# Scaling B and C of three chunk pairs on GpSimd instead of VectorE in a Mamba-2 plus low-rank-mixer kernel

## The chip, the cores and the metric

The kernel runs on one core of a Trainium2 chip. A core has five engines with a queue of instructions each: TensorE (PE in the profile; PEld is its weight load), VectorE (DVE), ScalarE (ACT), GpSimd (POOL) and SyncE (SP, which here only issues transfers). The engines run side by side and wait for one another by semaphores. The metric is the device time of one execution in microseconds (us); lower is better.

## The reference

The inputs are x (4 batches, 8 heads, 768 positions, 32 channels), decays a, and B and C (16 states per head). The first half is a chunked state-space scan; the second half a mixer on its output, as (batch, 768, 256).

```python
cum = np.cumsum(la, axis=-1)
L = np.exp(cum[:, :, :, None] - cum[:, :, None, :])
CB = np.einsum('bhin,bhjn->bhij', Cc, Bc)
M = CB * L * causal
y = M @ xc  +  (C @ state) * exp(cum)
state = exp(sum(la)) * state + sum_j B_j x_j exp(cum_last - cum_j)
...
h = xt @ U @ V
u = x + h.transpose(0, 2, 1)
out = u + np.maximum(u @ w_ch1, 0.0) @ w_ch2
```

The factor L splits: exp(cum_i - cum_j) is exp(cum_i - m) times exp(m - cum_j) for any m. So B may be multiplied by one factor for each position and head and C by another, and after that the masked product of the two is M.

## The kernel before

**Pairs.** The 768 positions of a batch are cut into 6 blocks of 128, taken two at a time: a *pair*. Pairs 0 to 2 belong to the first batch, 3 to 5 to the second, up to 11. For every pair the kernel does these steps, each a function of its own:

- `prep` (L344): the tile `BC` is B and C of the pair times the factors `F` (L271), which are computed for all positions ahead; 128 partitions by 512 columns, both inputs and the output in SBUF. It runs on VectorE. `BC` has two buffers.
- `decayed` (L356): `bd`, B times another factor `FD`, 128x256, on GpSimd.
- `turn` / `turning` (L374): four transposes of BC on TensorE, then ScalarE copies the result into `T` (L378) and, masked by head, `Cm` (L384).
- `gram` (L405): B times C in four PSUM banks of the tags x and z. `mask` (L417, VectorE) makes M of it.
- `state` (L438, TensorE) multiplies bd with x; `update` (L456, L458, VectorE) carries the state on, and L465 (GpSimd) makes `Sm` of it.
- `intra` (L537) and `inter` (L515) are the two products whose sum is y; `yout` (L549) copies y from PSUM.

**Weights.** The mixer's weights come in 64-bit floating point, as pairs of 32-bit words, and are converted piece by piece in `to_fp32`: on VectorE `e` (L315) and `top` (L317), on ScalarE `rest` (L319) and `power` (L321), and on VectorE again L323, L325 and L327 (the last writes the weight). Its scratch tiles have two buffers, so the first ScalarE step of one piece waits until L327 two pieces earlier has read that buffer. `convert_ahead` starts the next piece and then finishes the current one; its DVE order is L315, L317, L323, L325, L327.

**Mixer.** `up` (L701, then a ReLU on ScalarE, L706, into `gT`) and `down` (`whole`, L816) serve the first batch. Later batches use forms with fewer multiplications (L633 and L741). The `up` products use the same x and z banks as `gram`, so a gram has to wait until L706 has read them.

**Order.** The order on every engine is written out by hand: each queue runs its instructions as the program lists them. Pairs 0 to 2 are written out one by one; then the first batch's `up` pieces are interleaved with conversions and with the preparation of pairs 3 and 4:

```python
    prep(3)
    decayed(3)
    convert_ahead()
    ...
    turn(3)
    prep(4)
    decayed(4)
    ...
    gram(3); state(3); mask(3); update(3)
    convert_ahead()
```

From pair 3 on a loop does, for pair k: `prep(k + 2)`, `decayed(k + 2)`, then the mixer pieces of this turn with the four steps of `turning(k + 2)`, then `inter(k)`, `gram(k + 1)`, `intra(k)`, `state(k + 1)`, `mask(k + 1)` and so on. So pair 5 is prepared in the first turn of this loop, ahead of a `convert_ahead`.

SyncE issues all loads in one order fixed at the start. The input tiles `bc` and `x` have six buffers, so the load for pair 9 waits until the steps that read pair 3's tile are done.

Of the kernel before, what the change touches and what calls it, by code (L numbers as in the profile page):

```python
# [20 lines left out]
def kernel(  # L21
# [27 lines left out]
    nc = tc.nc  # L49
# [4 lines left out]
    NPR = NC // 2  # L54
# [284 lines left out]
    def prep(k, c=0, n=2):  # L339

        b, q = pairs[k]
        if c == 0:
            st[k] = {"BC": att.tile([P, 2, 2, NH, N], FP32, tag="BC", name="BC")}
        nc.vector.tensor_tensor(  # L344
            out=st[k]["BC"][:, :, c:c + n].rearrange("p i c h n -> p i (c h) n"),
            in0=bc_sb[k][:, :, c:c + n].rearrange("p i c h n -> p i (c h) n"),
            in1=F[:, :, b, 2 * q + c:2 * q + c + n].rearrange("p i c h -> p i (c h)")[
                :, :, :, None].to_broadcast([P, 2, n * NH, N]),
            op=ALU.mult)
# [555 lines left out]

    decays(one)
    prep(0, 0, 1)
    keep(one, "z")
    turn(0, 0, 1)
    prep(0, 1, 1)  # L910
    decayed(0)
    fill(1)
    turn(0, 1, 1, "w", nc.vector)
    fill(2)
    gram(0)
    prep(1, 0, 1)
    state(0)
    mask(0)
# [185 lines left out]
```

## Time and profile before

| what | us |
|---|---|
| median of 5 runs | 239.96 (239.7 to 241.28) |
| the profiled execution | 240.67 |
| its span, first to last instruction | 238.8 |
| TensorE busy in the span | 228.2 |
| VectorE busy | 155.4 |
| ScalarE busy | 95.5 |
| GpSimd busy | 20.5 |

All positions in the profile are us from the start of the span. The granted TensorE clock was 1.000 of full speed over the span. In a line of the timeline the first number is the start, the second the duration, then engine, source line and operation, output and inputs by the program's names, and in brackets how long the engine had been idle and what released it. An instruction may start a little ahead of the end of the one before it on the same engine. In the list of waits the three numbers are total, times and longest.

### The profile page before, as it was taken

The page shows a single profiled execution, that of the slowest core. Times are in us where ns is not written, and L with a number is a line of the kernel's source. Part 1 is how long each engine was busy: PE and PEld are TensorE (multiplying, and loading weights), DVE is VectorE, ACT ScalarE, POOL GpSimd, SP SyncE. Part 2 cuts the span into 40 slices and gives each one's busy share as a digit, 9 for nine tenths or more (in the row PEclk, how much of TensorE's full clock was granted, in tenths as well). Part 3 has the DMA queues.
Part 4 walks back from the last instruction along what each step waited for, and adds up shares of the span by engine and source line. Part 5 has one row for each costly group of instructions (what it writes and reads, how often), then busy time and mean ns, then how long its engine had stood idle before and what let it go on. Part 6 is the DMA issues. An engine that isn't in the chain of part 4 may idle for free.

```text
span 238.8 us, 7374 instructions
## 1 busy us (share of the span) xinstructions
PE 228.2 (96%) x3166; PEld 175.6 (74%) x3166; DVE 155.4 (65%) x363; ACT 95.5 (40%) x245; POOL 20.5 (9%) x40
## 2 busy tenths in 40 slices
PE   7988799897899999999999999999999999999995
PEld 5666566455688988565799987565799896559994
DVE  3675899798896666475896671556974372478511
ACT  5344647856414212537614112456312014663110
POOL 4221001120330300002021100010000000000000
PEclk9999999999999999999999999999999999999999
DMA  6975949998897830100001010000001011000111
GB/s 82 112 93 149 278 54 299 180 104 103 99 113 94 99 104 0 44 3 3 3 3 47 5 44 22 26 3 0 3 3 47 11 36 44 0 0 3 44 47 45
DMA packets 81909, 14.60 MB, mean 61 GB/s; under 512 B 76052, under 2 KB 80084, under 8 KB 81876
## 3 DMA queue, kind: packets, MB, share of 16 engines
q1 hardware_dynamic: 81876, 14.13, 32.5%
q8 instruction: 25, 0.41, 0.7%
q14 instruction: 8, 0.07, 0.1%
HBM read 10.98 MB, written 3.15 MB: 59 GB/s over the span
## 4 chain that ended last, share of the span: by engine, by line
PE 76%; SPq 10%; DVE 6%; DMA 3%; issue 2%; ACT 2%; DVEq 0%; ACTq 0%
PE x L741 17%; PE x L633 14%; PE z L741 13%; PE z L633 10%; SPq L117 8%; PE y L537 3%; PE x L816 3%; PE y L515 3%; PE x L405 2%; DMA words<-in_moe_w_ch_dram 2%; PE w L586 2%; PE w L557 2%; SPq L126 2%; PE x L737 1%; PE w L438 1%
## 5 line engine op out<-in xcount | busy, mean ns | idle before, releaser
L633 PE MATMUL x<-t,ws 128*128 128x384 f32 x72 | 28.7, 496 | 0.0
L741 PE MATMUL x<-w2s,words 128*128 128x128 f32 x176 | 23.2, 275 | 0.0
L741 PEld LDWEIGHTS x<-w2s,words 128*128 128x128 f32 x176 | 21.6, 193 | 0.0
L621 ACT ACTIVATE gT<-gT 128x384 f32<-128x384 f32 x36 | 19.0, 527 | 2.4 <-DVE gT L642 2.3
L465 POOL TENSOR_TENSOR Sm<-S,slot 128x256 f32<-128x256 f32 (+1 forms) x12 | 8.8, 735 | 121.4 <-DVE S L458 86.5
L633 PEld LDWEIGHTS x<-t,ws 128*128 128x128 f32 x72 | 12.5, 190 | 8.0 <-ACT top L638 1.3
L730 DVE TENSOR_TENSOR words<-gT 128x512 f32<-128x512 f32 (+1 forms) x28 | 16.7, 598 | 0.6 <-ACT gT L621 0.6
L642 DVE TENSOR_TENSOR gT<-z,top 128x384 f32<-128x384 f32 x12 | 6.7, 558 | 15.2 <-PE z L633 13.4
L638 ACT COPY e<-x 128x384 f32<-128x384 f32 x12 | 5.7, 478 | 23.2 <-PE x L633 23.2
L417 DVE TENSOR_TENSOR M<-x,causal 128x256 int32<-128x256 int32 x24 | 9.1, 420 | 9.0 <-PE z L405 7.7
L549 ACT COPY yT<-y 128x256 f32<-128x256 f32 x24 | 7.8, 375 | 16.5 <-PE y L515 16.5
L799 ACT COPY o<-x 128x128 f32<-128x128 f32 x11 | 2.9, 265 | 28.6 <-PE x L741 28.6
L405 PE MATMUL x<-Cm,T 32*64 32x128 f32 x192 | 11.9, 288 | 1.5 <-ACT Cm L384 1.1
L458 DVE SCALAR_TENSOR_TENSOR S<-S,kept,w 128x64 f32<-128x64 f32 x40 | 11.2, 279 | 3.1 <-PE w L438 1.4
L701 PE MATMUL x<-yT,w 128*128 128x384 f32 x32 | 12.0, 497 | 0.7 <-DVE yT L601 0.6
L741 PE MATMUL x<-w,gT 128*128 128x128 f32 x88 | 12.6, 286 | 0.0
L676 DVE TENSOR_SCALAR gT<-x 128x384 f32<-128x384 f32 x12 | 6.7, 557 | 9.1 <-PE x L633 9.1
L741 PEld LDWEIGHTS x<-w,gT 128*128 128x128 f32 x88 | 10.8, 191 | 2.3 <-issue 1.6
L741 PE MATMUL z<-w2s,words 128*128 128x128 f32 x88 | 11.9, 279 | 0.0
L356 POOL TENSOR_TENSOR bd<-bc,FD 128x256 f32<-128x256 f32 (+1 forms) x13 | 9.3, 716 | 30.3 <-ACT FD L282 16.3
L515 PE MATMUL y<-T,Sm 32*64 32x64 f32 x352 | 11.2, 230 | 0.7 <-ACT settled L471 0.4
L701 PE MATMUL z<-yT,w 128*128 128x384 f32 x32 | 11.6, 486 | 0.0
(179 smaller groups left out, 506.1 us busy)
## 6 DMA issues: line engine op xcount, KB each, us to landing
words<-in_moe_w_ch_dram SPq DMA_DIRECT2D x7, 512.0 KB, 6.0
x<-in_x_dram SPq DMA_DIRECT2D x24, 128.0 KB, 3.5
out_dram<-o SPq DMA_DIRECT2D x11, 256.0 KB, 2.1
bc<-in_B_dram SPq DMA_DIRECT2D x24, 64.0 KB, 3.4
bc<-in_C_dram SPq DMA_DIRECT2D x24, 64.0 KB, 2.9
words<-in_moe_w_ch_dram SPq DMA_DIRECT2D x2, 256.0 KB, 3.9
words<-in_moe_V_dram SPq DMA_DIRECT2D x1, 192.0 KB
words<-in_moe_U_dram SPq DMA_DIRECT2D x1, 192.0 KB, 5.0
```

Of the source, the lines that this page charges most:

```text
L117: nc.sync.dma_start(out=bc_sb[k][:, i, c], in_=src[b, :, ts(2 * q + c, P), :].rearrange("h s n -> s h n"))
L356: nc.gpsimd.tensor_tensor(out=st[k]["bd"][:, c:c + n].rearrange("p c h n -> p (c h) n"), in0=bc_sb[k][:, 0, c:c + n].rearrange("p c h n -> ...
L405: nc.tensor.matmul(out=g[r][cols, c], lhsT=s["T"][rows, 0, c, cols], rhs=s["Cm"][rows, :, c, cols], start=(c == 0), stop=True, skip_group_ ...
L417: done = nc.vector.tensor_tensor(out=M[:, r].bitcast(INT32).rearrange("p c s i -> p (c s) i"), in0=g[r].bitcast(INT32).rearrange("p c s i ...
L458: done = nc.vector.scalar_tensor_tensor(out=new, in0=st["S", b], scalar=kept[:, b, j, None], in1=add, op0=ALU.mult, op1=ALU.add)
L465: nc.gpsimd.tensor_tensor(out=s["Sm"][:, sl], in0=s["S"][:, sl].rearrange("p i (s d) -> p i s d", s=2), in1=slot[:, None, :, None].to_broa ...
L515: product = nc.tensor.matmul(out=y[p][ts(r % 2, H), r // 2, c], lhsT=own[ts(r, Q)], rhs=s["T"][ts(r, Q), 1, c, ts(p, H)], start=fresh(k, p ...
L621: nc.scalar.activation(g, g, AF.Relu)
L633: nc.tensor.matmul(out=X[name], lhsT=lhsT[:, ts(i, P)], rhs=rhs, start=start, stop=True, skip_group_check=True)
L701: nc.tensor.matmul(out=g, lhsT=w1[:, n, ts(m, P)], rhs=uT[:, n, ts(k, HS)], start=(n == 0), stop=(n == NCB - 1))
L730: nc.vector.tensor_tensor(out=S[v][:, lo:hi], in0=l[:, lo:hi], in1=r[:, lo:hi], op=op)
L741: nc.tensor.matmul(out=X[name], lhsT=lhsT[:, i], rhs=rhs[:, i], start=start and u is None and i == 0, stop=True, skip_group_check=True)
```

## The change

In `prep` the engine is chosen by the pair: pairs 3, 4 and 5 (`NPR` is 3), which are the second batch, use GpSimd, all others VectorE as before. The shapes, the values and the place in the program stay the same. On GpSimd's queue each of the three stands directly ahead of its pair's `bd`; on VectorE's queue three 128x512 instructions are gone. The source has one line more from there on, so L345 and later of the changed kernel are L344 and later of the kernel before.

```diff
         if c == 0:
             st[k] = {"BC": att.tile([P, 2, 2, NH, N], FP32, tag="BC", name="BC")}
-        nc.vector.tensor_tensor(
+        engine = nc.gpsimd if NPR <= k < NPR + 3 else nc.vector
+        engine.tensor_tensor(
             out=st[k]["BC"][:, :, c:c + n].rearrange("p i c h n -> p i (c h) n"),
             in0=bc_sb[k][:, :, c:c + n].rearrange("p i c h n -> p i (c h) n"),
             in1=F[:, :, b, 2 * q + c:2 * q + c + n].rearrange("p i c h -> p i (c h)")[
```

## The prediction

> **What bounds the kernel now.** I read the busy times first, then the chain of work that ended last, then what TensorE waited for, and last the timeline of the stretch in which the three edited instructions stand (38 to 57 us).
>
> The first and fourth part of the page:
>
> ```profile
> PE 228.2 (96%) x3166; PEld 175.6 (74%) x3166; DVE 155.4 (65%) x363; ACT 95.5 (40%) x245; POOL 20.5 (9%) x40
> ...
> PE 76%; SPq 10%; DVE 6%; DMA 3%; issue 2%; ACT 2%; DVEq 0%; ACTq 0%
> ```
>
> TensorE is the bound, and GpSimd is nearly empty. From about 57 us on, the chain is TensorE practically without a break, so time gained or lost on VectorE counts only where TensorE waits. Those places, from the list of its waits over the whole span:
>
> ```profile
> PE x L405 <- ACT Cm L384: 1.1, 1, 1.1
> PE x L374 <- DVE BC L344: 1.0, 3, 0.4
> ...
> PE w L374 <- DVE BC L344: 0.4, 1, 0.4
> ...
> PE x L405 <- ACT gT L706: 0.3, 1, 0.3
> ```
>
> The first is at 44.92 to 46.03 us (gram of pair 3), the third at 53.84 to 54.27 (turning of pair 5), the fourth at 55.38 to 55.65 (gram of pair 4); the second lies in the first batch and is not touched. So at most 0.43 + 0.27 = 0.70 us of waiting, 0.3% of the span, stands behind the edited lines; the 1.1 us hangs on a transfer, as the chain there shows:
>
> ```profile
> 35.26 4.69 DMA words<-in_moe_w_ch_dram
> 39.95 0.02 issue
> 39.97 0.43 DVE e L315
> ...
> 41.98 0.70 DVE w L327
> 42.68 0.02 issue
> 42.70 0.69 ACT rest L319
> ```
>
> And the timeline, VectorE, GpSimd and ScalarE, where the third edited instruction stands:
>
> ```profile
> 50.22 0.66 POOL L465 TENSOR_TENSOR Sm<-S,slot 128x256 f32<-128x256 f32 x1 [3.73 <-DVE S L458]
> 50.32 0.83 DVE L317 TENSOR_SCALAR top<-words 128x512 int32<-128x512 int32 x1
> 50.84 0.80 POOL L356 TENSOR_TENSOR bd<-bc,FD 128x256 f32<-128x256 f32 x1
> 51.08 1.10 DVE L323 SCALAR_TENSOR_TENSOR rest<-top,rest 128x512 f32<-128x512 f32 x1
> 52.11 0.69 DVE L325 SCALAR_TENSOR_TENSOR power<-words,power 128x512 int32<-128x512 int32 x1
> 52.83 0.69 DVE L327 SCALAR_TENSOR_TENSOR w<-rest,power 128x512 f32<-128x512 f32 x1
> 53.44 0.69 DVE L344 TENSOR_TENSOR BC<-bc,F 128x512 f32<-128x512 f32 x1
> 53.55 0.67 ACT L319 ACTIVATE rest<-words 128x512 f32<-128x512 uint32 x1
> 54.49 0.72 ACT L321 ACTIVATE power<-e,bias 128x512 int32<-128x512 int32 x1 [0.28 <-DVE e L315]
> ```
>
> The reader is to see that L317 takes 0.83 and L323 1.10 beside a running GpSimd instruction, where the same forms take 0.42 and 0.69 elsewhere. L323 ends at 52.18, so its own 0.69 began at 51.49, which is 0.15 before bd ended (51.64); bd in turn took 0.80 instead of 0.62 and began its own 0.62 at 51.02, just before L317 ended (51.15). Two such instructions do not run together: one waits until about 0.14 before the other's end. At 38.45 us a bd took its plain 0.62 beside L292 and L295 of VectorE, also at plain length, so some VectorE forms are free of this; the conversion's (L315 to L327) are not.
>
> **The change, part by part.** It takes three 128x512 instructions of L344 (0.68, 0.69, 0.69 us; the next one starts 0.60 after) off VectorE and puts them on GpSimd, each in front of its pair's bd. No transfer, matmul or ScalarE instruction moves. Loads queued on SyncE that reuse these input buffers (pair 9's first, at 66.12) wait for GpSimd alone instead of both, which has finished more than 20 us earlier: nothing.
>
> *Length on GpSimd.* No row shows 128x512. Bounds: 0.62 (a 128x256) and 2.12 (two 128x256 at the slowest seen, 1.06). GpSimd rows without a wait for the other engine are 0.40 for 128x128, 0.51 for 128x192, 0.62 for 128x256, a straight line of 0.11 per 64 columns; I take the line's 1.06 (an estimate), nearest to the rows.
>
> *Pair 3.* VectorE loses 39.00 to 39.68, but its next instruction waits for the transfer that lands at 39.95: gain 0, the idle time of 0.29 just grows. GpSimd can begin about 0.14 after F ends (37.83 + 0.30), at 38.27; BC ends 39.33, bd 39.95, lets go at about 39.81. TensorE wants BC at 41.74 and bd at 47.40: covered. L315 at 39.97 is on the chain above, so there are 0.16 us to spare. If the instruction takes D us instead of 1.06, this chain slips by D - 1.26 once D exceeds 1.26.
>
> *Pair 4.* VectorE loses 46.54 to 47.23; its next, the mask L417 at 47.49, waits for TensorE: gain 0. GpSimd: BC 46.54 to 47.60 (the C block lands just before), bd to 48.2. TensorE wants BC at 50.66 and bd at 57.29; Sm of pair 3 comes only at 50.22. If this cover were gone, each us late would be a us of TensorE's. Nothing.
>
> *Pair 5.* BC now stands between Sm and bd on GpSimd. The trace's landings put its last input at 50.85 (C's second block, issued by L117 at 48.39), so it starts when L317 lets go, 51.02, and ends 52.08. L323 waits to 51.94 and ends 52.63 (+0.45). bd waits for L323, 52.49 to 53.11; L325 now waits for bd to 52.97 and ends 53.66 (+0.86); L327 53.69 to 54.38 (was 53.52, +0.86). TensorE gets BC at 52.08, before it wants it, so the 0.43 goes. But ScalarE's L319 at 53.55 overwrites a buffer that L327 has just read (52.83 to 53.52, two buffers): it now waits to 54.41, L321 follows 0.60 later at 55.01 instead of 54.49, and the two gT behind it, which free the banks for the gram of pair 4, come 0.52 later. VectorE's L315, 0.60 earlier without BC and 0.86 later through the waits, comes at 54.30 and is no longer last. The gram starts 0.52 later, at 56.17; TensorE's old wait of 0.43 only moves into this one. If L323 wins the tie at 51.02 instead, BC runs 51.55 to 52.61, only L325 and then L327 wait, L327 ends 54.19, and the gram is 0.33 later. With D = 0.62, L327 slips 0.41 and the gram 0.07.
>
> The mask of pair 4, its state and update follow the gram, and TensorE behind them has no wait in which to win this back (the gaps at 57.70 and 64.12 are marked issue: 0.70 and 0.63, not data). **Sum:** 0 + 0 + 0.33 to 0.52; I take 0.5, since GpSimd's BC is ready before L323 (50.99 against 51.08). The profiled execution, 240.67 (its span 238.8 and 1.87 around it), would be 241.2; it stands 0.7 above the median 239.96, so for the median I say 240.45.
>
> *A rule against the change.* The Trainium skill, "GPSIMD Engine Reference", section "Engine selection", puts two-input elementwise work on VectorE and calls GpSimd about 2x slower; the rows here give 1.06 against 0.69, 1.5x. By the rule D would be about 1.35 (an estimate from that ratio and the 0.69), and the sum +0.9 in place of +0.5; no run here shows a 128x512 on GpSimd yet.
>
> **The rivals.**
> - *VectorE keeps its gain.* If GpSimd's waits do not reach the conversion, L327 still ends at 53.52, L319 starts at 53.55, L321 at 54.15 behind it, and the gram comes 0.34 earlier: 239.6. For it: BC is ready 2 us earlier and a 0.43 wait names it. Against it: L323's 1.10 beside bd in this very place. Its ceiling is the 0.70, so 0.5% (1.2 us) is out of its reach.
> - *Slower: the GpSimd instruction is long.* At D the sum is 0.52 + (D - 1.06) at pair 5, and above 1.26 another D - 1.26 at pair 3: 2D - 1.80. It decides, over 1.2 us, from D = 1.50. At D = 2.12 the bd of pair 3 no longer fits whole before L315, but falls behind it and delays L317: 0.69 there, and 0.52 + 1.06 at pair 5, so 2.3 in all: 242.2. For it: GpSimd rows of 1.00 and 1.06 exist for half the size. Against it: those began beside a VectorE instruction, and none runs beside the first two BC.
> - *Code position.* One row less for TensorE, three less for VectorE, three more for GpSimd move where the gaps marked issue fall. One such gap (0.63 to 0.70) more or less: 239.7 or 241.2 around my number.
> - *No effect.* The three are hidden on either engine: 240.0. This needs L319 to start at 53.55 as before, against the two-buffer order.
>
> **How the numbers follow.** Forecast with +0.07 to +0.9: 0.60. Gain kept, 0.10. No effect, 0.06. Long instruction, 0.13. Code position, 0.11. Against 0.5% (1.2 us, about what a measurement of this kernel can tell from no change): same holds the first three, less 0.02 of the kept gain (with one issue gap less it comes to 238.9, near the bound), and 0.06 of the code cases: 0.80. Slower: the long instruction and 0.03 of the code cases, 0.16. Faster: the 0.02 and the last 0.02 of the code cases, 0.04. The range from 239.4 (gain kept, less 0.2 for the spread of 239.7 to 240.0 seen below the median) to 241.6 (D about 1.7 by 2D - 1.80, past the point where that rival decides) leaves out the far end of the long instruction and stray runs.
>
> **What would show it.** Right: three L344 on GpSimd of about 1.06; L323 and L325 both near 1.1; L319 waiting for L327 at 54.4; TensorE's wait for BC of pair 5 gone and the one for gT grown to about 1; the first gram, near 46.03, unmoved. Wrong: L315 near 40 us stretched (pair 3's bd too late), L323 to L327 at 0.69 (gain kept), BC over 1.5 us, or a difference that arises after 60 us.

## The result and the profile after

The changed kernel takes 239.49 us (median of 45 runs, 238.11 to 246.77), the kernel before 239.96 (87 runs). The ratio is 0.999, with a 95% interval of 0.9976 to 1.0005: no difference that this measurement can tell. Some executions run some per cent longer, most of them at a lowered TensorE clock: ratios and intervals leave them out, medians keep them, and two profiles are of such executions, the first of the changed kernel (clock 0.965, span 244.8) and that of "pair 5 alone" (0.986). So the rows below are those of a second execution of the changed kernel (clock 0.999, span 237.5, time 239.47), and they are set beside a second profile of the kernel before from the same chip (span 237.4, time 239.29).

Parts 1 and 4 of the page of the changed kernel:

```profile
PE 228.2 (96%) x3166; PEld 176.1 (74%) x3166; DVE 154.3 (65%) x360; ACT 95.5 (40%) x245; POOL 24.1 (10%) x43
...
PE 80%; DVE 8%; SPq 5%; DMA 2%; ACT 2%; issue 1%; POOL 0%; DVEq 0%; POOLq 0%; ACTq 0%
```

Three instructions have moved from VectorE (363 to 360) to GpSimd (40 to 43), TensorE's busy time is the same 228.2, and GpSimd is still on the chain for 0%. VectorE has lost three instructions of 0.69, 2.1 us, and is only 0.8 us less busy than in the second profile of the kernel before (155.1; 1.1 less than in the first): the rest went into waits, which count as busy.

Where they went, pair 5, GpSimd and then VectorE and ScalarE (start, duration, engine and line, output and inputs, idle time before with its releaser):

```profile
50.03 0.66 POOL L466 TENSOR_TENSOR Sm<-S,slot 128x256 f32<-128x256 f32 x1 [2.05 <-DVE S L459]
50.65 1.23 POOL L345 TENSOR_TENSOR BC<-bc,F 128x512 f32<-128x512 f32 x1
51.85 1.07 POOL L357 TENSOR_TENSOR bd<-bc,FD 128x256 f32<-128x256 f32 x1
...
50.14 0.84 DVE L317 TENSOR_SCALAR top<-words 128x512 int32<-128x512 int32 x1
50.90 1.54 DVE L323 SCALAR_TENSOR_TENSOR rest<-top,rest 128x512 f32<-128x512 f32 x1
52.36 1.11 DVE L325 SCALAR_TENSOR_TENSOR power<-words,power 128x512 int32<-128x512 int32 x1
53.50 0.69 DVE L327 SCALAR_TENSOR_TENSOR w<-rest,power 128x512 f32<-128x512 f32 x1
...
54.23 0.68 ACT L319 ACTIVATE rest<-words 128x512 f32<-128x512 uint32 x1 [0.76 <-DVE w L327]
54.81 0.71 ACT L321 ACTIVATE power<-e,bias 128x512 int32<-128x512 int32 x1
55.42 0.47 ACT L707 ACTIVATE gT<-x 128x384 f32<-128x384 f32 x1
```

The two engines take turns: L317 is held by Sm, BC by L317 (1.23 instead of the 1.06 of pairs 3 and 4), L323 by BC (1.54 instead of 0.69), bd by L323 (1.07 instead of 0.62), L325 by bd (1.11 instead of 0.69). L327 is free again, and ScalarE's L319 waits for it to 54.23. What TensorE waited for, changed kernel (engine, line, releaser: total, times, longest):

```profile
PE x L406 <- ACT gT L707: 1.4, 1, 1.4
PE x L406 <- ACT Cm L385: 0.8, 1, 0.8
...
PE y L538 <- issue: 0.2, 1, 0.2
```

And the kernel before, second profile:

```profile
PE x L405 <- ACT Cm L384: 0.7, 1, 0.7
...
PE w L374 <- DVE BC L344: 0.4, 1, 0.4
...
PE y L537 <- issue: 0.4, 1, 0.4
PE w L438 <- issue: 0.3, 1, 0.3
PE x L405 <- ACT gT L706: 0.3, 1, 0.3
```

The wait for BC of pair 5 is gone, and the one for gT has grown from 0.3 to 1.4. So far this is the forecast. But in the same list two gaps of TensorE marked issue are gone as well. The chain of the kernel before, at those two places:

```profile
56.89 0.22 PE w L438 x11
57.11 0.28 issue
57.40 0.42 PE w L438 x21
...
62.70 0.41 PE y L537 x29
63.11 0.35 issue
63.47 0.54 PE y L537 x34
```

The chain of the changed kernel, at the same products:

```profile
57.78 0.37 PE w L439 x29
...
63.04 0.79 PE y L538 x50
```

The chain takes a few products less on one side than on the other, so I compare whole groups, from the start of the first product to the start of the last: the 32 state products (L438) take 0.89 us broken by a gap and 0.35 unbroken, the 64 y products 1.16 and 0.64. So the gaps cost 0.54 and 0.52, more than their issue rows say.

I cut the stretch that differs into two stages by TensorE's starts: from the gram of pair 3 to the gram of pair 4 (its first product that waits for gT), and from there to the first weight load of `whole` (L816 before, L817 after). Kernel before, second profile: 9.61 and 9.73. Changed kernel: 10.10 and 8.72. That is +0.49 and -1.01, so the stretch is 0.5 us *shorter* in the profile, where the prediction has +0.5.

The stages on either side show no such step: the first gram starts at 45.05 to 46.34 us and the rest from `whole` to the end takes 172.57 to 173.02 in all profiles at full clock, whichever the kernel. The time of an execution less its span, as a median over all executions of a call, is 1.85 us for the kernel before and 1.97 for the changed one (1.86 and 1.98 in the comparison on another chip below, and 2.12 for "pairs 3 and 4 alone"): 0.1 us that no view of the profile places.

### The profile page after: what moved, and what is told of

Its sections match the earlier page's. It is cut to its first block, busy times and chain, and to the rows that moved or that the text cites. A ratio compares the mean times of both kernels' runs of the same rounds, so it can differ in the third digit from the quotient of the medians.

```text
span 244.8 us, 7374 instructions
## 1 busy us (share of the span) xinstructions
PE 232.2 (95%) x3166; PEld 178.5 (73%) x3166; DVE 156.1 (64%) x360; ACT 95.6 (39%) x245; POOL 24.9 (10%) x43
## 4 chain that ended last, share of the span: by engine, by line
PE 80%; DVE 9%; SPq 5%; ACT 2%; issue 2%; DMA 1%; DVEq 0%; ACTq 0%
PE x L742 17%; PE x L634 13%; PE z L742 12%; PE z L634 9%; PE y L538 4%; SPq L117 4%; PE y L516 4%; PE x L817 3%; PE x L406 2%; PE w L558 2%; PE w L587 2%; PE w L439 1%; DVE rest L323 1%; DVE power L325 1%; DVE w L327 1%
## 5 line engine op out<-in xcount | busy, mean ns | idle before, releaser
L702 PE MATMUL x<-yT,w 128*128 128x384 f32 x32 | 12.5, 515 | 0.7 <-DVE yT L602 0.6
L516 PE MATMUL y<-T,Sm 32*64 32x64 f32 x352 | 12.4, 250 | 0.7 <-ACT settled L472 0.4
L516 PEld LDWEIGHTS y<-T,Sm 32*64 32x64 f32 x352 | 8.7, 148 | 4.4 <-issue 2.1
L406 PEld LDWEIGHTS x<-Cm,T 32*64 32x64 f32 x192 | 7.6, 137 | 5.7 <-ACT Cm L385 2.3
```

The lines of the kernel that those rows point to most:

```text
L406: nc.tensor.matmul(out=g[r][cols, c], lhsT=s["T"][rows, 0, c, cols], rhs=s["Cm"][rows, :, c, cols], start=(c == 0), stop=True, skip_group_ ...
L516: product = nc.tensor.matmul(out=y[p][ts(r % 2, H), r // 2, c], lhsT=own[ts(r, Q)], rhs=s["T"][ts(r, Q), 1, c, ts(p, H)], start=fresh(k, p ...
L702: nc.tensor.matmul(out=g, lhsT=w1[:, n, ts(m, P)], rhs=uT[:, n, ts(k, HS)], start=(n == 0), stop=(n == NCB - 1))
```

## The experiments

Every kernel's median is over 12 executions, set beside the kernel before on the same chip (medians 239.86, 239.53, 239.12 and 240.06 in the four comparisons; 239.55, 238.88, 238.88 and 239.99 over the executions that the ratios use). All stages in this section are those defined above.

**Both kernels again.** No edit; a further profile and time of each.

> The changed kernel once more, for a profile at full clock. Both theories agree on one stretch: from the first mask of pair 3 to the first product of pair 4's gram that waits for gT it takes 8.64 us, as in the first profile of the changed kernel, where the kernel before has 8.16. They differ on what follows, the stretch from that product to the first L817 product of the mixer (10.52 us before, 55.65 to 66.17). Theory 1, the prediction's: it stays at 10.5 and the time is 0.5 us over the kernel before. Theory 2: TensorE's gaps marked issue (0.70 and 0.63 before, each 256 TensorE instructions after the other) are waits for its next block of instructions, which come by the same DMA engines as the data; a later gram finds the block loaded, so the stretch shrinks by 0.5 to 1.3 and the time is 0 to 0.8 us below. Theory 3: the waits of VectorE belonged to that one profile; then the first stretch is near 8.16.

> The kernel before once more, for a second profile. Theory 2 expects the gaps marked issue at the same two instructions (in state of pair 4 and in intra of pair 4) but of a length that varies with when the block's transfer ran, 0 to 1 us each; theory 1 takes them as part of the code and expects 0.70 and 0.63 again. Time: no difference beyond 0.2 per cent.

The changed kernel: 239.73, ratio 0.9997 (0.9964 to 1.0030). The kernel before, against other runs of itself: 239.04, ratio 0.9971 (0.9944 to 0.9998). So a comparison of this size can be 0.3% off with no change at all, and its interval can miss 1. Everything below that goes by times alone has to be read with that; the stages of the profiles repeat to about 0.05 us where no gap falls.

**Pair 5 alone, and pairs 3 and 4 alone.**

```diff
-        engine = nc.gpsimd if NPR <= k < NPR + 3 else nc.vector
+        engine = nc.gpsimd if k == NPR + 2 else nc.vector          # pair 5 alone
+        engine = nc.gpsimd if NPR <= k < NPR + 2 else nc.vector    # pairs 3 and 4 alone
```

> Only pair 5 is scaled on GpSimd. If the prediction is right that pairs 3 and 4 cost and bring nothing, everything is as with all three: L323 about 1.5 and L325 about 1.1 us, first stretch 8.64 us. Theory 1: time 0.5 us over before. Theory 2: the same as after_again, within 0.3 us. Rival (the gain comes from pairs 3 and 4): slower than after_again by 0.3 us or more.

> Only pairs 3 and 4 are scaled on GpSimd. Prediction: no effect, first stretch 8.16 us, TensorE waits 0.4 us for pair 5's BC on VectorE as before, L315 near 40 us at 0.42 us, time within 0.2 us of before. Theory 2 leaves it the gaps marked issue as before, since TensorE's position in time is not changed: 0 to 1 us each. Rival (gain from pairs 3 and 4): as fast as after_again while only5 is not.

Pair 5 alone: 239.57, ratio 0.9997 (0.9964 to 1.0031), stages 10.10 and 8.66, as the whole change. Pairs 3 and 4 alone: 239.77, ratio 0.9979 (0.9942 to 1.0016), stages 9.61 and 10.08, as the kernel before, with its gaps and its waits. From its list of TensorE's waits:

```profile
PE w L439 <- issue: 0.7, 1, 0.7
...
PE w L375 <- DVE BC L345: 0.4, 1, 0.4
...
PE y L538 <- issue: 0.3, 1, 0.3
PE x L406 <- ACT gT L707: 0.3, 1, 0.3
```

So both the +0.49 and the lost gaps come from pair 5. TensorE issues 6381 instructions in "pair 5 alone" and in the kernel before, so the number of its instructions does not explain that the gaps are gone there.

What are the gaps? In every profile that has both, they begin exactly 256 TensorE instructions apart, and the page's DMA part lists a queue of its own, "q8 instruction", with 25 packets of 16 KB; TensorE issues 6381 instructions, which 25 blocks of 256 just hold. I read such a gap as a wait for the next block of TensorE's own program. The packets bear this out: in all seven gaps of the 14 profiles (two each before the change, in its repeat and in "pairs 3 and 4 alone", one in the last run below) TensorE goes on 1.25 to 1.45 us after the end of the latest packet, and at the 21 places without a gap it comes to the new block 1.76 us or more after it. (The Trainium skill, "Advanced Engine Details and Errata", section "ISA Cache", gives a cache line as 16 KB, 256 instructions; the packets and the distance of the gaps here agree with it.) The next question was why the block came late in one kernel and in time in the other. The DMA view of the kernel before, 54 to 57.5 us:

```profile
q8 instruction: 1, 0.02, 2.2%
```

and of the changed kernel, 50.5 to 54 us:

```profile
q8 instruction: 1, 0.02, 2.6%
```

Each has one packet there and none in the other's window: the block is fetched at 54.89 us before and at 51.36 after. What lies ahead of it on TensorE's queue is the wait of `turning` for pair 5. By source line, the separate wait instructions ("EVENT_SEMAPHORE" on the queue of the weight loads; first and last start), kernel before:

```profile
L374 PEldq EVENT_SEMAPHORE  x2: 51/51/51, 49.2 to 53.6; - x2
```

Changed kernel:

```profile
L375 PEldq EVENT_SEMAPHORE  x2: 51/51/51, 49.6 to 49.9; - x2
```

Before, the queue stands at that instruction until VectorE has made BC (53.57 us). After, it passes at 49.92: the wait for GpSimd's BC sits on the weight load itself, and what is left in the separate instruction has long been met. My theory was now that a queue held at a separate wait fetches late. Rivals: the block comes when it comes, and the later gram alone hides it; or the packet is slowed by data transfers. The last is not borne out by the packets' own length: 0.92 to 1.47 us where the block came early, 0.93 to 1.36 where it came late. Whether data transfers delay the start of a packet, no run here tells.

**An idle product ahead of the four transposes.** The kernel uses such products elsewhere; one here takes over the separate wait of the turning, so BC's wait moves onto the weight load, with BC on VectorE as before.

```diff
+        if k == NPR + 2:
+            fill(1)
         tp = bank(tag, 2, n, P)
```

> The kernel before (all scaling on VectorE) with one idle product of TensorE ahead of pair 5's transposes, into the same bank. The profiles show that a wait for two engines stands on TensorE's queue as an instruction of its own (EVENT_SEMAPHORE), and before the change it holds the queue at pair 5's transposes until VectorE's BC ends (53.57 in the second profile of before); only then does the queue reach the point where the next block of 256 instructions is fetched. The idle product takes the early wait, and the wait for BC alone sits on the transpose itself. Theory 2 refined (late queue, late fetch): the fetch that ran at 55 to 56 us runs 3 us earlier, the gaps marked issue after it fall below 0.2, gram of pair 3 to gram of pair 4 stays 9.61, from there to the first L817 product goes from 9.7-10.4 to 8.7-9.1, time 0.6 to 1.2 us under before. Theory 2 as first put (a later gram hides the fetch): gaps stay, time as before. Theory 1: no effect.

> The changed kernel with the same idle product, as the control for late_seq. Theory 2 refined: no effect, since TensorE's queue already runs ahead here: 10.10 from gram to gram, 8.7 from there to the mixer's first L817 product, no gap marked issue over 0.35. Time within 0.2 us of the changed kernel.

On the kernel before: 238.54, ratio 0.9979 (0.9950 to 1.0008); stages 9.60 and 8.67. The gaps are gone without the move to GpSimd, and without the +0.49. The block is fetched at 51.30, in the DMA view of 50.5 to 54 us:

```profile
q8 instruction: 1, 0.02, 1.8%
```

On the changed kernel: 238.98, ratio 0.9992 (0.9965 to 1.0020); stages 10.13 and 8.69, as without the product, which has nothing left to win there. Between the two kernels, on one chip, the medians stand 0.44 apart (0.50 over the executions that the ratios use), the size of the +0.5 of the gram, though the intervals overlap.

**The queue held on purpose.** In the changed kernel an idle product that waits for L325 of the conversion, ahead of the same transposes; and in the kernel before, an idle product that itself waits for BC of pair 5 (so nothing but the idle product's presence differs from the kernel before). Both write to a part of the bank that the first transpose overwrites.

```diff
+            first = nc.tensor.matmul(out=tp[:, 0, 0], lhsT=ident, rhs=ident, start=True, stop=True)
+            tc.add_manual_dep(first.ins, powers[-2].ins.name, ...)     # L325; the changed kernel
+            tc.add_manual_dep(first.ins, s["scaled"].ins.name, ...)    # BC; the kernel before
```

> As after_fill5, but the idle product also waits for VectorE's L325 of the conversion that GpSimd holds up (it ends at 53.46 in the second profile of the changed kernel). This holds TensorE's queue about as long as before the change, while BC stays on GpSimd and the gram of pair 4, which starts at 55.9, waits no longer than it did. Theory 2 refined: the fetch goes back to 55 us or later, gaps marked issue come back (together 0.4 to 1.3), from gram of pair 4 to the first L817 product 9.3 to 10.4, time 0.4 to 1.3 us over after_fill5: this is the 0.5 us slower kernel that was predicted. Theory that the later gram alone hides the fetch: no change against after_fill5.

> The control for fill5: the same idle product in the kernel before, all scaling on VectorE, but the idle product itself waits for pair 5's BC, so TensorE's queue is held until VectorE's BC ends, as in the kernel before, and the gram of pair 4 is not later. Theory 2 refined: the gaps marked issue are back (together 0.4 to 1.3), the fetch at 54.8 us or later, from gram of pair 4 to the first L817 product 9.5 to 10.4, gram to gram 9.6, time as before and 0.5 to 1 us over fill5. Rival (the idle product itself, by moving the instructions' positions, made fill5 what it is): as fill5, 8.7.

The changed kernel with the held queue: 239.00, ratio 0.9991 (0.9960 to 1.0022); stages 10.12 and 8.67. The queue passes at 53.64, and the block is fetched late, at 54.78, seen in the view of 54 to 57.5 us:

```profile
q8 instruction: 1, 0.02, 2.4%
```

The late fetch is as the theory says, but the gaps that it forecast do not follow: the gram itself comes 0.5 later, and TensorE starts the first product of the new block at 57.89, 1.76 us after the packet's end, with nothing to wait for. So the later gram alone can hide the first gap. It can hide no more than the 0.5 us by which it is later, though, and this queue was held 0.5 us less than before the change (7.66 against 8.13 in the table below). The kernel before with the held queue: 238.99, ratio 0.9974 (0.9945 to 1.0003); stages 9.61 and 8.67. The queue passes at 53.27, as late as before, but the block was already fetched at 50.64, and there is no gap. That goes against the theory, and it is what the rival on record forecast (as fill5, 8.7): that the idle product itself, by moving the instructions' positions, took the gaps away.

**The gram later still.** A second, unused scaling of pair 5 on GpSimd between BC and bd.

```diff
+        if k == NPR + 2:
+            extra = att.tile([P, 2, 2, NH, N], FP32, tag="extra", name="extra", bufs=1)
+            nc.gpsimd.tensor_tensor(out=extra..., in0=bc_sb[k]..., in1=F..., op=ALU.mult)
```

> The changed kernel with pair 5's scaling done twice on GpSimd (the second result is not used). If the two engines exclude each other as read, L323, L325 and L327 take 1.54, 1.54 and 1.10 us, gram to gram goes from 10.10 to 10.94, and since no gap is left to hide it, the time is 0.8 us over the changed kernel. If a later gram is always hidden, time within 0.2 us of the changed kernel.

240.15, ratio 1.0050 (1.0009 to 1.0091); stages 10.84 and 8.67. VectorE's conversion:

```profile
50.31 1.54 DVE L323 SCALAR_TENSOR_TENSOR rest<-top,rest 128x512 f32<-128x512 f32 x1
51.78 1.54 DVE L325 SCALAR_TENSOR_TENSOR power<-words,power 128x512 int32<-128x512 int32 x1
53.36 0.99 DVE L327 SCALAR_TENSOR_TENSOR w<-rest,power 128x512 f32<-128x512 f32 x1
```

And GpSimd's:

```profile
50.07 1.24 POOL L345 TENSOR_TENSOR BC<-bc,F 128x512 f32<-128x512 f32 x1
51.27 1.50 POOL L354 TENSOR_TENSOR extra<-bc,F 128x512 f32<-128x512 f32 x1
52.74 1.06 POOL L366 TENSOR_TENSOR bd<-bc,FD 128x256 f32<-128x256 f32 x1
```

Now L325 is held by the extra instruction to 1.54, as L323 by BC, and L327 by bd to 0.99. The gram slips by another 0.74, the second stage has no gap left to give back, and the time is up, with an interval that lies just above 1.

**Second runs of three kernels**, for the intervals and for the exception above.

> fill5 once more, for its time. From its profile, 0.9 to 1.7 us less than the kernel before in the stretch from gram of pair 3 to the mixer; the time should be 0.3 to 0.5 per cent under before if that holds in most executions, and within 0.2 if the gaps of before are mostly shorter than in its profiles.

> The changed kernel once more, for its time and a third profile: 10.10 us gram to gram, 8.7 from there to the mixer, sum 18.8. By the stretches of the profiles (19.3 to 20.0 before) 0.5 to 1.2 us under before; by the times so far 0 to 0.5.

> fill5_late once more. Its first profile had TensorE's queue held to 53.27 and yet an early fetch (50.64) and no gaps, against theory 2 refined. If fetches come early or late by chance from one execution to the next, this profile may show the late fetch (about 54.5) and gaps of 0.4 to 1.3, 9.1 to 10.4 from gram of pair 4 to the mixer. If the code decides, it is as in the first profile: 8.67, and the held queue is not the cause.

The idle product alone: 238.39, ratio 0.9983 (0.9945 to 1.0020); stages 9.61 and 8.67. The changed kernel: 239.75, ratio 1.0035 (1.0001 to 1.0068); stages 10.11 and 8.69. The held idle product: 239.26, ratio 0.9976 (0.9954 to 0.9997); stages 9.61 and 8.95. This time the block was fetched late, at 54.38, TensorE came to it at 56.66, just too early, and the stage is 0.28 longer. That is one short gap; the forecast by the theory was 9.1 to 10.4, and the rival's 8.67 is not met either.

All profiles together. The wait passed, and the start of the packet, are us from the start of the gram of pair 3 in the same profile (differences of starts in the trace):

| kernel | queue passes the wait | block fetched | gram 3 to gram 4 | gram 4 to whole | both |
|---|---|---|---|---|---|
| before | 8.13 | 9.95 | 9.61 | 10.42 | 20.03 |
| before, again | 8.13 | 9.45 | 9.61 | 9.73 | 19.34 |
| pairs 3 and 4 | 8.13 | 10.05 | 9.61 | 10.08 | 19.69 |
| changed, again | 4.07 | 5.51 | 10.10 | 8.72 | 18.82 |
| changed, third | 4.08 | 5.42 | 10.11 | 8.69 | 18.80 |
| pair 5 | 4.08 | 5.76 | 10.10 | 8.66 | 18.76 |
| idle product | 4.08 | 6.07 | 9.60 | 8.67 | 18.27 |
| idle product, again | 4.08 | 4.88 | 9.61 | 8.67 | 18.28 |
| changed and idle product | 4.09 | 5.85 | 10.13 | 8.69 | 18.82 |
| second scaling | 4.08 | 5.79 | 10.84 | 8.67 | 19.51 |
| changed, held | 7.66 | 8.80 | 10.12 | 8.67 | 18.79 |
| before, held product | 8.12 | 5.49 | 9.61 | 8.67 | 18.27 |
| the same, again | 8.12 | 9.33 | 9.61 | 8.95 | 18.56 |

The fetch falls at 4.9 to 6.1 or at 8.8 to 10.0, nowhere between. With the queue let through at 4.1 it is early in seven profiles of seven; with the queue held it is late in five of six.

**What stays open.** That the held wait goes with the late fetch is shown; that it decides it is not, for one held queue had an early fetch, and what else has a say was not found. Counted back 256 instructions from the gap, the block before begins only some six instructions ahead of the held wait in the order of the trace, and these rows do not tell which of the two the fetch goes by.

The second gap is open altogether. It stands only in the three profiles with the stretch unchanged, where the second block's packet starts 15.4 to 16.5 us after the gram of pair 3; in the others it starts at 12.4 to 13.9, also in the two whose first block came late (13.6 in the changed kernel with the held queue, 13.8 in the repeat of the held product). So a late first block does not by itself bring the second gap. With the idle product in place, holding the queue brought back 0 and 0.28 us of the 1.06 to 1.75 that the gaps cost in those three profiles, and the rival of the moved positions is not excluded for the kernels with an idle product.

Nor does the time settle what the profiles say of the sum. They give the changed kernel 0.5 to 1.2 us less than the kernel before in this stretch; the three comparisons of times give 0.999, 0.9997 and 1.0035. A part is the 0.1 us outside the span; whether the executions without a profile have their gaps as often as the three profiles with that stretch unchanged, no run here can show. The second scaling suggests that they have less of them: its stretch of 19.51 lies within the 19.34 to 20.03 of the kernel before, yet its time is 0.5% longer (0.1 to 0.9). And no version is clearly better than both: the idle product alone has the lowest medians (238.54 and 238.39), but its intervals reach over 1, and the kernel before differed from itself by as much.

## Why the prediction was right, and which step was not

The forecast of 240.45, no change that can be told, holds: 239.49 lies in its range, 0.96 below the forecast and 0.09 above the range's lower end. Part of that is luck: the forecast had the +0.5 of the gram and not the gaps that went with it, and the two happen to be of like size. The +0.5 itself did not show in the time (a ratio of 1.002, above the interval that ends at 1.0005). By its steps:

- *The length on GpSimd.* 1.06 us for 128x512, as the straight line through the smaller rows had it: 1.06 at pair 3 and at pair 4, and at pair 5 1.23 with 0.17 of waiting. The ratio to VectorE's 0.69 is 1.5, so the long instruction is refuted. (Its 2D - 1.80 has a slip of 0.04: with 0.16 us to spare at pair 3 the chain slips by D - 1.22, not D - 1.26.) (The 2x of the Trainium skill, "GPSIMD Engine Reference", section "Engine selection", is too high for this form; the smaller rows of the trace were the better source.)
- *Pair 5.* L323, L325, L327, L319, L321 and gT each slipped as laid out: L323 takes 1.54 (51.08 to 52.63, 1.55, in that working, though the signs listed behind it have "both near 1.1"), L325 1.11 beside bd, L327 its plain 0.69, and the gram of pair 4 came 0.49 later after the gram of pair 3 (0.52 forecast), alike in six profiles (10.10 to 10.13 against 9.60 to 9.61). The wait for gT is 1.4 instead of about 1, with BC's 0.43 moved into it. The second scaling confirms the rule behind it: one instruction more on GpSimd, one more conversion instruction at 1.54.
- *The gain kept* is refuted by the same rows: GpSimd's waits do reach the conversion.
- *Pair 4.* Nothing, as forecast: BC and bd are over at 47.99, and no wait names them.
- *Pair 3.* The number, nothing, was right, the reason was not. The transfer landed earlier in this execution, and the 0.16 us to spare were not there: bd held L315. VectorE and then GpSimd, changed kernel:

```profile
38.29 0.43 DVE L292 TENSOR_TENSOR own<-w,mine 128x264 f32<-128x264 f32 x1
38.76 0.43 DVE L295 TENSOR_REDUCE kept<-own 128x33 f32<-128x264 f32 x1
39.43 0.79 DVE L315 TENSOR_SCALAR e<-words 128x512 int32<-128x512 int32 x1 [0.25 <-DMA words<-in_moe_w_ch_dram]
...
38.30 1.06 POOL L345 TENSOR_TENSOR BC<-bc,F 128x512 f32<-128x512 f32 x1 [16.53 <-ACT F L271]
39.32 0.62 POOL L357 TENSOR_TENSOR bd<-bc,FD 128x256 f32<-128x256 f32 x1
```

  L315 takes 0.79 instead of 0.42: its own 0.42 begins at 39.80, 0.14 before bd ends. But without BC in front of it VectorE is ready for it earlier. Where the transfer came early, it is 2.26 to 2.28 us from L292's start to L317's end in three profiles with BC on GpSimd and 2.12 in two (pairs 3 and 4 alone, second scaling), where L315 went ahead of bd; with BC on VectorE it is 2.15 to 2.16 in five. Where the transfer came late, it is 2.54 before and 2.67 in the changed kernel with the held queue. So +0.1 at most, and 0.04 less in two. The stretched L315 is one of the signs of being wrong that the forecast listed; its cost was covered.
- *The step that failed* is "TensorE behind them has no wait in which to win this back (the gaps at 57.70 and 64.12 are marked issue: 0.70 and 0.63, not data)". The gaps were taken as fixed, because no engine is named in them. They were waits for the kernel's own instructions (1.25 to 1.45 us behind a packet's end, each time), and with pair 5 on GpSimd they are gone: -1.01 in the second stage beside the +0.49 in the first. Two things changed there, the queue let through and the gram later, and the later gram alone can hide up to 0.5 us of the first gap; why the second goes with it is not shown. The rival of the code position named these gaps and their size, but as chance; for the move of pair 5 the three profiles with the gaps and the five without speak against chance, for the kernels with an idle product it still stands. The second gap also meets the forecast's own sign of being wrong, "a difference that arises after 60 us". In the time, the two about cancel, within what it can tell.

## What to carry to other kernels

A gap marked issue on the bounding engine is not a constant: look at the instruction queue's packets beside it, and at what the engine's sequencer stood still for in the microseconds before. Two-input work moved to GpSimd did not run in parallel with this kernel's conversion on VectorE, though it did with L292 and L295: look in the trace which forms take turns, reckon whole instructions in turn there, and follow what the delayed VectorE instruction frees. And measure the kernel against itself first: here that alone gave 0.9971 with an interval that missed 1.

## What the runs showed of the hardware that was not expected

- TensorE's program comes in blocks of 256 instructions (16 KB packets, 25 of them). A block that comes late stops TensorE until 1.25 to 1.45 us after its packet's end, with issue rows of 0.06 to 0.70 us; with the products on both sides of the gap it is 0.5 us each at rows of 0.28 and 0.35.
- In this stretch of all 14 profiles the data transfers pause behind such a packet. In the second profile of the kernel before, behind the packet that ends at 56.14, the DMA engines' busy share is 0.10 from 56.6 to 57.3 us, against 0.94 from 55 to 56 and full again from 57.5; with the idle product, behind the one that ends at 52.33, it is 0.10 from 52.4 to 53.4.
- Which wait stands alone on the queue and which sits on the instruction itself depended on the engine waited for: VectorE's BC was waited for in a separate instruction (queue passes at 8.13 after the gram of pair 3), GpSimd's on the weight load (4.07), with no more and no fewer TensorE instructions in "pair 5 alone" than before. Behind a separate wait that held, the block came about 3 to 5 us later in five of six profiles.
- GpSimd's two-input multiplication from SBUF: 0.40 for 128x128, 0.62 for 128x256, 1.06 for 128x512, against VectorE's 0.69 for the last.
